# A two-attention kernel: V of the second attention in 4096 B rows, quads in pairs, one PSUM pool

## The chip, the core and the metric

The kernel runs on one core of a Trainium2 chip. Its time is the device time of that core in microseconds. The times and the profile are those of the kernel before the change.

## What is computed

Two attention blocks over cached keys and values, independent of each other, with their outputs side by side. All data are bf16.

```python
def _A_ref(x, k_cache, v_cache, wq, wo):      # x 16x32x1024, 32 query heads, 4 key/value heads, Sk 1024, Dh 128
    q = (x @ wq).reshape(B, Sq, Hq, Dh).transpose(0, 2, 1, 3)
    k = jnp.repeat(k_cache, rep, axis=1)      # rep = 8
    v = jnp.repeat(v_cache, rep, axis=1)
    scores = jnp.einsum("bhqd,bhkd->bhqk", q, k) * (Dh ** -0.5)
    p = softmax(scores, axis=-1)
    o = jnp.einsum("bhqk,bhkd->bhqd", p, v)
    return o.transpose(0, 2, 1, 3).reshape(B, Sq, Hq * Dh) @ wo
# _B_ref: the same with 32 key/value heads (no repeat)
return jnp.concatenate([a, b], axis=-1)
```

The second attention (B) reads K and V of 16 batches x 32 heads x 1024 x 128, 134 MB each; the first one (A) reads an eighth of that.

## The kernel before

**Quads.** Both attentions are cut into 128 units of 128 query rows, called quads. A quad of A is four heads of one batch that share K and V. A quad of B is two batches (`q.b0`, `q.b0 + 1`) times two heads (`q.h0`, `q.h0 + 1`), 32 queries each. For every quad the kernel makes scores into two PSUM banks, the negated row maximum (`st_max`, L866, DVE), the exponential with its sum (`st_exp`, L879, ACT), the transpose of P by TensorE with two bf16 taken as one fp32 (`st_ptr`, L891), its copy into `PT_sb` (`st_pev`, L540), the product with V (`st_pv`, L913 for A, L921 for B), the normalizing copy into `O_sb` (`st_norm`, L937 on ACT, L938 on DVE), a transpose of O (`st_otr`, L943) and its copy into `OTA_sb` or `OTB_sb` (L540). Query projections (L624, L643), the shuffling of B's queries into `QR` (L667) and the output projections (L712, added up by L723 and L726) run between the quads.

**B's K.** A tile `KB_sb` holds two heads of one batch: a partition has 16 consecutive keys, one row of 4096 B from memory (`st_dmaK`, L781). DVE transposes it in place in 32x32 blocks (`st_ktrB`, L815). Because of this layout the scores are made of 32x32 tiles of the matmul array, four passes of eight matmuls for each quad (L856): the row group is head and half (`rg = 2 * hh + g2`), the column group is batch and head (`cg = 2 * t_ + hh`). There are 8 K slots.

**B's V.** A V load (`st_dmaV`, L794) takes two heads of one batch with 8 consecutive keys to a partition and head, so a row from memory has 2048 B. A quad needs two such loads; there are 3 slots of two loads. In the product a stationary tile is 32 queries wide (128 rows x 32 columns, four column groups), the moving operand is one 128-key chunk of V, 128 columns.

**PSUM.** Two pairs of banks are for scores, taken in turn (`ps_s`); four banks are for everything else (`ps_g`), and two of them are kept for projections where possible.

**Order.** The program first lists all operations with what they read and write. `list_schedule` then plays them through with the durations in `DUR`, a model of the DMA queue (`PACKET`, `DMA_ISSUE`, `SP_AHEAD`), the slots in `SLOTS` and a priority made of the longest path and the step number; the order in which it starts the operations is the order in which each engine's instructions are written out. At run time there are only in-order engines and semaphores. All loads go through SP's queue, in one order; a load whose slot isn't free holds back all loads behind it. `evac` copies may go to ACT or DVE, as the planner chooses (`any`).

The main loop adds one quad of B (`quadB_all`) and about one of A (`quadA_all`) at each of 128 steps. `quadB_all` adds V's loads for the quad three ahead and K's loads for the quad four ahead.

Of the kernel before, what the change touches and what calls it, by code (L numbers as in the profile page):

```python
# [16 lines left out]
NVB_SLOTS = 3  # L17
NQT = 7
# [10 lines left out]
PE_MODE = {"scoresB": 2, "Qshuf": 2, "Qshuf2": 2, "PVB": 1}  # L29
MODE_SWITCH = 0.05  # L30
LOOK = 0.35
STEP_US = 3
STEP_NEAR = 0
TAIL_STEP = 123
# [11 lines left out]
    "scoresB": (0.216, 0.20), "scoresA": (0.216, 0.20), "PT_trA": (0.49, 0.22), "PT_trB": (0.49, 0.22), "PVA": (0.45, 0.22), "PVB": (0.112, 0.22),  # L46
    "OT_tr": (0.056, 0.22), "KTA_tr": (0.45, 0.22), "Qshuf": (0.15, 0.20), "Qshuf2": (0.15, 0.20), "qprojA": (0.432, 0.20), "qprojB": (0.432, 0.20),
    "oprojA": (0.432, 0.20), "oprojB": (0.432, 0.20), "xT_tr": (0.45, 0.22),
    "exp": (1.10, 0.12), "PT_ev@act": (0.466, 0.13), "norm@act": (0.25, 0.13), "OT_ev@act": (0.11, 0.13), "KTA_ev@act": (0.466, 0.13),
    "qA_ev@act": (0.47, 0.13), "qB_ev@act": (0.478, 0.13), "QR_ev@act": (0.478, 0.13), "acc0@act": (0.47, 0.13), "acc0@dve": (0.58, 0.12), "xT_ev@act": (0.90, 0.13),  # L50
    "o_fin@act": (0.47, 0.13),
    "KBt_tr": (1.126, 0.11), "max": (1.12, 0.11), "recip": (0.06, 0.11), "norm@dve": (0.23, 0.13), "PT_ev@dve": (0.58, 0.12),
    "OT_ev@dve": (0.08, 0.12), "KTA_ev@dve": (0.58, 0.12), "QBt_tr": (0.345, 0.10), "acc+": (0.58, 0.12), "accF": (0.59, 0.12),
# [4 lines left out]
PACKET = {"kb_dma": (4096, 0.159), "wqh_dma": (1024, 0.049)}  # L58
PACKET_DEFAULT = (2048, 0.084)
# [40 lines left out]
SLOTS = {"bank": 4, "P": 3, "PT": 3, "stat": 6, "O": 2}  # L100
BANK_RESERVE = {"pj": 2}


def actual(res):
    out = []
    for r in res:
        if not isinstance(r, Virt):
            out.append(r)
        elif r.cls == "bank":
            out.append(("bank", 4 + r.idx))  # L110
        else:
            out.append((r.cls, r.idx))
    return tuple(out)


class Prog:
# [118 lines left out]
    def list_schedule(self, lat=0.05, look=LOOK):  # L235
# [48 lines left out]

        def slot_time(i):

            t = 0.0
            for k_, v in enumerate(acq[i]):
                nth = sum(1 for w in acq[i][:k_] if w.cls == v.cls)
                idle = [slot_free[v.cls][x] for x in range(SLOTS[v.cls]) if held[v.cls][x] is None]  # L290
                keep = sum(k for kind, k in BANK_RESERVE.items() if kind != v.kind and not any(h is not None and h.kind == kind for h in held["bank"])) if v.cls == "bank" else 0
                if len(idle) <= keep + nth:
                    return None
                t = max(t, sorted(idle)[nth])
            return t

        def acquire(i, st):
            for v in acq[i]:
                x = min((x for x in range(SLOTS[v.cls]) if held[v.cls][x] is None), key=lambda x: slot_free[v.cls][x])
                held[v.cls][x] = v  # L300
                v.idx = x
# [25 lines left out]

        def occ(i, eng):
            return dict(ops[i].alts)[eng] if ops[i].alts else ops[i].dur
        while True:  # L330
            best = None
            bkey = None
            for eng, lst in ready.items():
# [11 lines left out]
                for i in lst:  # L345
                    s_ = slot_time(i) if acq[i] else 0.0
                    if s_ is not None:
                        at[i] = max(ready_t[i], fe, s_) + sw(i)
                if not at:
                    continue  # L350
                emin = min(at.values())
                cand = [i for i in at if at[i] <= emin + look]
# [21 lines left out]
            if op.dma_key is not None:  # L374
                free[beng] = st + DMA_ISSUE
                xs = max(st + DMA_FIRST, dma_free[0])
                dma_free[0] = xs + dma_time(op)
                op.t1 = dma_free[0] + DMA_LAST
            else:
                oc, tl = occ(best, beng)  # L380
                free[beng] = st + oc
                op.t1 = st + oc + tl
# [67 lines left out]
def build(nc, pa, pb, out):  # L450
# [34 lines left out]
    with stack:  # L485
# [21 lines left out]
        VB_sb = sb("VB_sb", [P, NVB, 2, 2, NCH, Dh], BF)  # L507
# [3 lines left out]
        P_sb = sb("P_sb", [P, SLOTS["P"], Sk], BF)  # L511
        PT_sb = sb("PT_sb", [P, SLOTS["PT"], NCH, P], BF)
        O_sb = sb("O_sb", [P, SLOTS["O"], Dh], BF)

        ps_s = ps("ps_s", [P, 2, 2, 512], F32)
        ps_g = ps("ps_g", [P, 4, 512], F32)

        def bank(v):
            return ps_g[:, v.idx, :]

        def bankb(v):
            return ps_g[:, v.idx, :].bitcast(BF)
# [229 lines left out]
        def mk_quadB(t):  # L752
# [7 lines left out]
            q.hp = jb % 2  # L760
            q.b0 = 4 * q.G + 2 * q.bp
            q.h0 = q.m * MS + 2 * q.hp
            q.ks = [(2 * t + t_) % NKB for t_ in range(2)]
            q.vslot = t % NVB
# [6 lines left out]
        def st_dmaK(q, t_=None):  # L771
            if q.pi == 0:
                if not q.kv_new:
                    return
                sl = q.kvslot
                pr.add("sp", lambda e: e.dma_start(KA_sb[:, sl, :, :], pa["k"][q.b, q.s].rearrange("(p c) d -> p c d", c=NCH)),
                       writes=[("KA", sl)], dma_key=f"ka{sl}", name="ka_dma", dur=Sk * Dh * 2, wtag={("KA", sl): q.kid})
            else:
                sl = q.ks[t_]
                ksrc = pb["k"][q.b0 + t_, q.h0:q.h0 + 2].rearrange("hh (p s) d -> (hh p) (s d)", s=16)  # L780
                pr.add("sp", lambda e: e.dma_start(KB_sb[:, sl, :], ksrc), writes=[("KB", sl)], dma_key=f"kb{sl}", name="kb_dma", dur=2 * Sk * Dh * 2, wtag={("KB", sl): q.kid})  # L781

        def st_dmaV(q):
            if q.pi == 0:
                if not q.kv_new:
                    return
                sl = q.kvslot
                pr.add("sp", lambda e: e.dma_start(VA_sb[:, sl, :, :], pa["v"][q.b, q.s].rearrange("(p c) d -> p c d", c=NCH)),
                       writes=[("VA", sl)], dma_key=f"va{sl}", name="va_dma", dur=Sk * Dh * 2, wtag={("VA", sl): q.kid})
            else:  # L790
                sl = q.vslot
                for t_ in range(2):
                    vsrc = pb["v"][q.b0 + t_, q.h0:q.h0 + 2].rearrange("hh (p c) d -> p hh c d", c=NCH)
                    pr.add("sp", lambda e, t_=t_, vsrc=vsrc: e.dma_start(VB_sb[:, sl, t_, :, :, :], vsrc), writes=[("VB", sl, t_)],  # L794
                           dma_key=f"vb{sl}_{t_}", name="vb_dma", dur=2 * Sk * Dh * 2, wtag={("VB", sl, t_): q.kid})
# [17 lines left out]
        def st_ktrB(q, t_):  # L813
            sl = q.ks[t_]
            pr.add("dve", lambda e: e.transpose(KB_sb[:, sl, :].bitcast(F32), KB_sb[:, sl, :].bitcast(F32)),  # L815
                   writes=[("KB", sl)], name="KBt_tr", rtag={("KB", sl): q.kid}, wtag={("KB", sl): ("T", q.kid)})

        s_rr = [0]

        class SBuf:  # L820
            def __init__(self, idx):
                self.idx = idx
                self.res = [("bank", 2 * idx), ("bank", 2 * idx + 1)]

        def st_scores(q):
            q.vS = SBuf(s_rr[0] % 2)
            s_rr[0] += 1
            q.vP, q.vPT, q.vst, q.vO = Virt("P"), Virt("PT"), Virt("stat"), Virt("O")
            q.vbt, q.vbo = Virt("bank"), Virt("bank")
            vS = q.vS  # L830
            if q.pi == 0:
# [3 lines left out]
                for u in range(2):  # L835
                    pr.add("pe", lambda e, u=u: e.matmul(ps_s[:, vS.idx, u, :], qt[:, q.b, q.hh0:q.hh0 + 4, :].rearrange("p a q -> p (a q)"),  # L836
                                                         KTA_sb[:, sl, u * 512:(u + 1) * 512], start=True, stop=True),
                           reads=[("QT", q.s % 2, q.hh0 + a) for a in range(4)] + [("KTA", sl)], writes=vS.res, name="scoresA", dur=0.225,
                           tag="A%d" % q.t, rtag=dict([(("QT", q.s % 2, q.hh0 + a), q.s) for a in range(4)] + [(("KTA", sl), q.kid)]))
            else:  # L840
                gp = (q.m * NG + q.G) % 2

                def e_s(e, fp):
                    last = None
                    if True:
                        f, pd = fp // 2, fp % 2
                        o0 = f * 64 + pd
                        for t_ in range(2):
                            a = 2 * q.bp + t_
                            for hh in range(2):  # L850
                                cg = 2 * t_ + hh
                                for g2 in range(2):
                                    rg = 2 * hh + g2
                                    lhsT = QR[32 * rg:32 * rg + 32, gp, a, q.hp, o0:o0 + 63:2]
                                    rhs = KB_sb[32 * rg:32 * rg + 32, q.ks[t_], :].rearrange("p (s x) -> p s x", s=16)[:, :, o0:o0 + 63:2]
                                    last = e.matmul(ps_s[32 * cg:32 * cg + 32, vS.idx, g2, :].rearrange("p (s j) -> p s j", s=16), lhsT, rhs,  # L856
                                                    start=(fp == 0), stop=(fp == 3), tile_position=(32 * rg, 32 * cg))
                    return last
                for fp_ in range(4):
# [296 lines left out]
```

## Time and profile before

| | |
|---|---|
| time, median of 3 runs (lowest to highest) | 888.49 us (888.01 to 891.52) |
| profiled execution: its own time, its span | 888.67 us, 886.9 us |
| granted TensorE clock | 0.994 |
| PE, DVE, ACT busy | 798.9 us (90%), 733.0 (83%), 612.1 (69%) |
| bytes moved by DMA, mean rate | 341.65 MB, 385 GB/s |
| DMA packets | 144830 |
| loads of B's V, of B's K | 256 x 512 KB each, issued by SP |

The span runs from the first to the last instruction; the time has 1.8 us around it. Busy shares are unions of an engine's instructions, and overlapping matmuls count once. PEld is TensorE's weight load. "SPq" in waits is SP's queue of DMA issues. A wait is given as who waited, at which line, for whom, with the sum in us, the number of times and the longest.

### The profile page before, as it was taken

The page shows a single profiled execution, that of the slowest core. Times are in us where ns is not written, and L with a number is a line of the kernel's source. Part 1 is how long each engine was busy: PE and PEld are TensorE (multiplying, and loading weights), DVE is VectorE, ACT ScalarE, POOL GpSimd, SP SyncE. Part 2 cuts the span into 40 slices and gives each one's busy share as a digit, 9 for nine tenths or more (in the row PEclk, how much of TensorE's full clock was granted, in tenths as well). Part 3 has the DMA queues.
Part 4 walks back from the last instruction along what each step waited for, and adds up shares of the span by engine and source line. Part 5 has one row for each costly group of instructions (what it writes and reads, how often), then busy time and mean ns, then how long its engine had stood idle before and what let it go on. Part 6 is the DMA issues. An engine that isn't in the chain of part 4 may idle for free.

```text
span 886.9 us, 29149 instructions
## 1 busy us (share of the span) xinstructions
PE 798.9 (90%) x12699; PEld 468.8 (53%) x12864; DVE 733.0 (83%) x1020; ACT 612.1 (69%) x1357; POOL 5.0 (1%) x15
## 2 busy tenths in 40 slices
PE   7999899998999999999999989998999877987976
PEld 3455555555555555555555555555555544554643
DVE  0498987979887888998898879887889888998985
ACT  3486886667777575767768666686667766676763
POOL 0000000000000000000000000000000000000000
PEclk9999999999999999999999999999999999999999
DMA  9999999999999999999999999999999999999995
GB/s 331 397 395 393 392 393 396 393 394 392 395 377 384 393 395 394 392 392 394 395 364 394 393 392 396 394 394 387 396 395 377 392 395 395 376 395 393 397 397 200
DMA packets 144830, 341.65 MB, mean 385 GB/s; under 512 B 12032, under 2 KB 12032, under 8 KB 144704
## 3 DMA queue, kind: packets, MB, share of 16 engines
q1 hardware_dynamic: 144144, 337.95, 100.6%
q8 instruction: 101, 1.65, 0.8%
q0 software_dynamic: 560, 1.84, 0.5%
q14 instruction: 25, 0.20, 0.1%
HBM read 337.64 MB, written 2.10 MB: 383 GB/s over the span
## 4 chain that ended last, share of the span: by engine, by line
PE 49%; DMA 21%; DVE 13%; ACT 11%; SPq 3%; issue 3%; DVEq 0%; ACTq 0%
DMA KB_sb<-in_B_k_cache_dram 14%; PE ps_s L856 11%; PE ps_g L712 9%; PE ps_g L891 8%; ACT P_sb L879 7%; DVE stat L866 6%; DVE KB_sb L815 5%; DMA VA_sb<-in_A_v_cache_dram 5%; PE ps_g L921 4%; PE ps_g L624 4%; PE ps_g L913 4%; PE ps_g L643 3%; PE ps_s L836 2%; ACT PT_sb L540 2%; PE ps_g L943 2%
## 5 line engine op out<-in xcount | busy, mean ns | idle before, releaser
L866 DVE TENSOR_REDUCE stat<-ps_s 128x1 f32<-128x1024 f32 x256 | 305.5, 1209 | 56.1 <-PE ps_s L856 49.8
L815 DVE STREAM_TRANSPOSE KB_sb<-KB_sb 128x1024 f32<-128x1024 f32 x256 | 309.3, 1228 | 38.0 <-DMA KB_sb<-in_B_k_cache_dram 36.3
L879 ACT ACTIVATE P_sb<-ps_s,stat 128x1024 bf16<-128x1024 f32 x256 | 285.8, 1118 | 55.3 <-DVE stat L866 53.4
L891 PE MATMUL ps_g<-id,P_sb 128*128 128x128 f32 x1024 | 172.4, 296 | 13.6 <-ACT OTA_sb L540 5.7
L856 PE MATMUL ps_s<-KB_sb,QR 32*32 32x512 bf16 x4096 | 160.9, 397 | 17.9 <-ACT P_sb L879 13.9
L891 PEld LDWEIGHTS ps_g<-id,P_sb 128*128 128x128 f32 x1024 | 148.7, 207 | 49.6 <-ACT OTA_sb L540 8.7
L540 ACT COPY PT_sb<-ps_g 128x512 f32<-128x512 f32 x235 | 136.2, 591 | 44.9 <-PE ps_g L891 43.8
L937 ACT ACTIVATE O_sb<-ps_g,stat 128x128 bf16<-128x128 f32 x193 | 70.1, 371 | 67.8 <-PE ps_g L921 40.5
L921 PE MATMUL ps_g<-VB_sb,PT_sb 128*32 128x128 bf16 x4096 | 90.6, 222 | 5.7 <-ACT PT_sb L540 1.7
L856 PEld LDWEIGHTS ps_s<-KB_sb,QR 32*32 32x32 bf16 x4096 | 48.2, 89 | 77.2 <-ACT P_sb L879 21.0
L921 PEld LDWEIGHTS ps_g<-VB_sb,PT_sb 128*32 128x32 bf16 x4096 | 59.7, 97 | 52.1 <-issue 37.5
L913 PE MATMUL ps_g<-VA_sb,PT_sb 128*128 128x128 bf16 x1024 | 78.6, 221 | 5.8 <-DMA VA_sb<-in_A_v_cache_dram 2.8
L913 PEld LDWEIGHTS ps_g<-VA_sb,PT_sb 128*128 128x128 bf16 x1024 | 61.0, 98 | 35.2 <-issue 14.6
L643 PE MATMUL ps_g<-wq_sb,xT_sb 128*128 128x512 bf16 x230 | 68.2, 393 | 5.2 <-DMA wq_sb<-in_B_wq_dram 2.3
L712 PE MATMUL ps_g<-woB_sb,OTB_sb 128*128 128x512 bf16 x230 | 62.6, 380 | 8.8 <-ACT OTB_sb L540 2.3
L836 PE MATMUL ps_s<-KTA_sb,QT_sb 128*128 128x512 bf16 x180 | 64.2, 385 | 5.4 <-ACT O_sb L937 2.6
L712 PE MATMUL ps_g<-woA_sb,OTA_sb 128*128 128x512 bf16 x238 | 59.0, 380 | 4.0 <-issue 1.7
L943 PE MATMUL ps_g<-ident,O_sb 128*128 128x128 bf16 x256 | 51.5, 223 | 8.3 <-ACT O_sb L937 4.4
L879 ACT ACTIVATION_READ_ACCUMULATOR P_sb<-ps_s,stat 128x1 f32 x256 | 51.4, 201 | 0.0
L624 PE MATMUL ps_g<-xT_sb,wq_sb 128*128 128x512 bf16 x174 | 49.1, 380 | 2.0 <-issue 1.0
L540 ACT COPY OTA_sb<-ps_g 128x64 f32<-128x64 f32 x120 | 25.7, 214 | 33.2 <-PE ps_g L943 32.5
L723 DVE TENSOR_TENSOR acc<-acc,ps_g 128x512 f32<-128x512 f32 x64 | 40.8, 673 | 9.1 <-PE ps_g L712 8.9
(44 smaller groups left out, 511.6 us busy)
## 6 DMA issues: line engine op xcount, KB each, us to landing
VB_sb<-in_B_v_cache_dram SPq DMA_DIRECT2D x256, 512.0 KB, 12.2
KB_sb<-in_B_k_cache_dram SPq DMA_DIRECT2D x256, 512.0 KB, 12.4
KA_sb<-in_A_k_cache_dram SPq DMA_DIRECT2D x64, 256.0 KB, 12.3
VA_sb<-in_A_v_cache_dram SPq DMA_DIRECT2D x64, 256.0 KB, 12.2
wq_sb<-in_B_wq_dram SPq DMA_DIRECT2D x16, 512.0 KB, 12.1
woB_sb<-in_B_wo_dram SPq DMA_DIRECT2D x32, 256.0 KB, 11.2
woA_sb<-in_A_wo_dram SPq DMA_DIRECT2D x32, 256.0 KB, 9.9
wq_sb<-in_A_wq_dram SPq DMA_DIRECT2D x12, 512.0 KB, 12.6
```

The costliest lines, as they stand in the source:

```text
L540: return e.copy(dst, src) if hasattr(e, "activation") else e.tensor_copy(dst, src)
L624: last = e.matmul(bank(v)[:, 0:tn], w_[:, j, hh * Dh:(hh + 1) * Dh], xT_sb[:, 0, j, t0:t0 + tn], start=(j == 0), stop=(j == DJ - 1))
L643: last = e.matmul(bank(v)[:, 0:CW], xT_sb[:, 1, j, G * P:(G + 1) * P], wq_sb[:, j, mh * CW:(mh + 1) * CW], start=(j == 0), stop=(j == DJ - 1))
L712: last = e.matmul(bank(v)[:, 0:OUTW], OT[:, gp, hh, :], wo_[:, hh, oh * OUTW:(oh + 1) * OUTW], start=(hh == 0), stop=(hh == nh - 1))
L815: pr.add("dve", lambda e: e.transpose(KB_sb[:, sl, :].bitcast(F32), KB_sb[:, sl, :].bitcast(F32)), writes=[("KB", sl)], name="KBt_tr", rta ...
L836: pr.add("pe", lambda e, u=u: e.matmul(ps_s[:, vS.idx, u, :], qt[:, q.b, q.hh0:q.hh0 + 4, :].rearrange("p a q -> p (a q)"), KTA_sb[:, sl, ...
L856: last = e.matmul(ps_s[32 * cg:32 * cg + 32, vS.idx, g2, :].rearrange("p (s j) -> p s j", s=16), lhsT, rhs, start=(fp == 0), stop=(fp == 3 ...
L866: pr.add("dve", lambda e: e.tensor_reduce(stat[:, vst.idx, 0:1], ps_s[:, vS.idx, :, :], AXIS.XY, ALU.max, negate=True), writes=vS.res + [v ...
L879: return e.activation(dst, src, ACTF.Exp, bias=stat[:, vst.idx, 0:1], scale=1.0, accum_out=stat[:, vst.idx, 1:2])
L891: last = e.transpose(bank(vb)[:, m * P:(m + 1) * P], p32[:, m:Sk // 2:NPK], id32[:])
L913: last = e.matmul(bank(vb)[:, 0:Dh], ptc_of(vPT, c, 0, P), VA_sb[:, kvs, c, :], start=(c == 0), stop=(c == NCH - 1))
L921: last = e.matmul(bank(vb)[32 * a:32 * a + 32, 0:Dh], ptc_of(vPT, c, 32 * a, 32 * a + 32), VB_sb[:, kvs, a // 2, a % 2, c, :], start=(c == ...
```

## The change

- **V of B.** A V load now has K's layout: two heads of one batch, 16 consecutive keys to a partition, one row of 4096 B. The number of loads (256) and their size (512 KB) stay. A V tile thus holds two heads of equal place on different halves of the partitions (64 partitions a head).
- **Pairs.** Two quads that follow each other become a pair with a common set of four K tiles and four V tiles. The quads of a pair no longer split the heads as (0,1) and (2,3): `q.e` is the parity, and a quad has heads `e` and `2 + e` of both batches. The scores of both quads are one operation of four passes of 16 matmuls, each on a 32x32 tile of its own. The exponentials of both quads go into one tile `P2_sb`; its eight transposes give two PT copies into `PT2_sb`; the product with V takes 64 matmuls of 64x64 tiles whose moving operand is 256 columns wide (two V tiles side by side).
- **Turning O back.** Each quad's result now holds, for each row, both heads of a parity, of which half is wanted. `st_norm` copies 256 columns instead of 128, and the transpose becomes two matmuls with `rowsel`, a selecting identity that POOL fills at the start. The copy into `OTB_sb` is 128 columns of bf16 instead of 64 fp32 words.
- **Slots.** V: 6 slots of one load, filled behind the pair's product (`pairB`). P2 and PT2 have one slot each, O2 three; P and PT go from 3 to 2, `stat` from 6 to 8, the projected queries (`NQT`) from 7 to 5.
- **PSUM.** One pool of 8 banks; scores take banks in neighbouring pairs, at most 6 at a time; a pair of quads takes four at once.
- **Planner.** New durations, a larger cost for a change of the array's tiling, a model of instruction blocks that PE has to fetch, and rules for placing banks (`place`).

```diff
-NVB_SLOTS = 3
-NQT = 7
+NVB_SLOTS = 6
+NQT = 5
...
-SLOTS = {"bank": 4, "P": 3, "PT": 3, "stat": 6, "O": 2}
-BANK_RESERVE = {"pj": 2}
+SLOTS = {"bank": 8, "P": 2, "P2": 1, "PT": 2, "PT2": 1, "stat": 8, "O": 2, "O2": 3}
...
-        VB_sb = sb("VB_sb", [P, NVB, 2, 2, NCH, Dh], BF)
+        VB_sb = sb("VB_sb", [P, NVB, 16, Dh], BF)
...
-        ps_s = ps("ps_s", [P, 2, 2, 512], F32)
-        ps_g = ps("ps_g", [P, 4, 512], F32)
+        psum = ps("psum", [P, 8, 512], F32)
...
+        pr.add("pool", lambda g: g.memset(rowsel[:], 0.0), writes=["rowsel"], name="c0")
+        for r_ in range(4):
+            pr.add("pool", lambda g, r_=r_: g.tensor_copy(rowsel[32 * r_:32 * r_ + 32, r_ % 2, 32 * r_:32 * r_ + 32], ident[32 * r_:32 * r_ + 32, 32 * r_:32 * r_ + 32]),
+                   reads=["ident"], writes=["rowsel"], name="c1")
...
-                for t_ in range(2):
-                    vsrc = pb["v"][q.b0 + t_, q.h0:q.h0 + 2].rearrange("hh (p c) d -> p hh c d", c=NCH)
+        def tile_src(key, x):
+            q, i = quadsB[2 * (x // 4)], x % 4
+            h = q.m * MS + 2 * (i % 2)
+            return pb[key][q.b0 + i // 2, h:h + 2].rearrange("e (p s) d -> (e p) (s d)", s=16)
...
+        def st_scoresB(qs):
...
+                for x in range(4):
+                    for q in qs:
+                        for g2 in range(2):
+                            r0 = 32 * (2 * q.e + g2)
+                            lhsT = QR[r0:r0 + 32, gp, 2 * q.bp + x // 2, x % 2, o0:o0 + 63:2]
+                            rhs = KB_sb[r0:r0 + 32, q.ks[x], :].rearrange("p (s x) -> p s x", s=16)[:, :, o0:o0 + 63:2]
+                            last = e.matmul(bank(q.vS[g2])[32 * x:32 * x + 32, :].rearrange("p (s j) -> p s j", s=16), lhsT, rhs,
+                                            start=(fp == 0), stop=(fp == 3), tile_position=(r0, 32 * x))
...
+        def st_pvB(qs):
...
+                for c in range(c0, c0 + 4):
+                    for t_ in range(2):
+                        s0 = q0.vs[2 * t_]
...
+                        for q in qs:
+                            e0, n0 = 64 * q.e, 64 * t_
+                            last = e.matmul(bank(q.vbo)[n0:n0 + 64, 0:2 * Dh].rearrange("p (i d) -> p i d", i=2), pt[e0:e0 + 64, c // 2, n0:n0 + 64, c % 2],
+                                            VB_sb[e0:e0 + 64, s0:s0 + 2, c, :], start=(c == 0), stop=(c == 15), tile_position=(e0, n0))
...
+                def e_ot(e):
+                    for i in range(2):
+                        last = e.matmul(bank(vb)[:, 256:384], O2_sb[:, vO.idx, i, :], rowsel[:, i, :], start=(i == 0), stop=(i == 1))
...
+        def pairB(n):
+            qs = [quadsB[2 * n], quadsB[2 * n + 1]]
+            for x in range(4):
+                st_ktrB(4 * n + x)
...
+            st_scoresB(qs)
+            for x in range(4):
+                st_dmaKB(4 * n + NKB + x)
+            for q in qs:
+                st_max(q)
+                st_exp(q)
+            st_ptB(qs)
+            st_pvB(qs)
+            for x in range(4):
+                st_dmaVB(4 * n + NVB + x)
+            for q in qs:
+                st_recip(q)
+                st_norm(q)
+                st_otr(q)
```

More of the change, by code (lines that the diff above doesn't have):

```diff
@@ L285, in slot_time @@
         def slot_time(i):
-            t = 0.0
+            got = place(i)
+            if got is None:
+                return None
+            t = got[1]
             for k_, v in enumerate(acq[i]):
[L289 to L294, printed above, removed]
+                if v.cls != "bank":
+                    nth = sum(1 for w in acq[i][:k_] if w.cls == v.cls)
+                    idle = [slot_free[v.cls][x] for x in range(SLOTS[v.cls]) if held[v.cls][x] is None]
+                    if len(idle) <= nth:
+                        return None
+                    t = max(t, sorted(idle)[nth])
@@ L295, in slot_time @@
             return t
         def acquire(i, st):
+            got = iter(place(i)[0])
             for v in acq[i]:
-                x = min((x for x in range(SLOTS[v.cls]) if held[v.cls][x] is None), key=lambda x: slot_free[v.cls][x])
+                if v.cls == "bank":
+                    x = next(got)
+                else:
+                    x = min((x for x in range(SLOTS[v.cls]) if held[v.cls][x] is None), key=lambda x: slot_free[v.cls][x])
                 held[v.cls][x] = v
@@ L332, in list_schedule @@
             bkey = None
+            waiting = [i for i in ready.get("pe", ()) if banks_of(i) > 1 and ready_t[i] <= free.get("pe", 0.0) + HOLD_AHEAD]
+            big[0] = max(waiting, key=lambda i: bl[i]) if waiting else None
             for eng, lst in ready.items():
@@ L769, in mk_quadB @@
             return q
[L771 to L781, printed above, removed]
@@ L839, in st_scores @@
                            tag="A%d" % q.t, rtag=dict([(("QT", q.s % 2, q.hh0 + a), q.s) for a in range(4)] + [(("KTA", sl), q.kid)]))
[L840 to L859, printed above, removed]
-                    pr.add("pe", lambda e, fp_=fp_: e_s(e, fp_), reads=[("QR", gp, 2 * q.bp), ("QR", gp, 2 * q.bp + 1), ("KB", q.ks[0]), ("KB", q.ks[1])],
-                           writes=vS.res, name="scoresB", dur=0.275, tag="B%d" % q.t,
-                           rtag={("QR", gp, 2 * q.bp): (q.m, q.G), ("QR", gp, 2 * q.bp + 1): (q.m, q.G), ("KB", q.ks[0]): ("T", q.kid), ("KB", q.ks[1]): ("T", q.kid)})
@@ L864, in st_max @@
         def st_max(q):
             vS, vst = q.vS, q.vst
-            pr.add("dve", lambda e: e.tensor_reduce(stat[:, vst.idx, 0:1], ps_s[:, vS.idx, :, :], AXIS.XY, ALU.max, negate=True),
-                   writes=vS.res + [vst], name="max")
+            pr.add("dve", lambda e: e.tensor_reduce(stat[:, vst.idx, 0:1], both(vS), AXIS.XY, ALU.max, negate=True),
+                   writes=vS + [vst], name="max")
         def st_exp(q):
```

346 lines of the change are left out of this document (218 added, 128 removed).

## The prediction

> **What bounds the kernel now.** I read the page's 40 slices first, then SP's part of the timeline at the start and the windows beside it, then the groups, SP's own waits and the end of the timeline.
>
> The slices: the 16 DMA engines are full in all but the last, at 364 to 397 GB/s.
>
> ```profile
> DMA  9999999999999999999999999999999999999995
> GB/s 331 397 395 393 392 393 396 393 394 392 395 377 384 393 395 394 392 392 394 395 364 394 393 392 396 394 394 387 396 395 377 392 395 395 376 395 393 397 397 200
> ```
>
> PE (90% busy) and DVE (83%) are close behind, and the chain that ended last gives DMA only 21%; but a chain passes through whichever engine releases a buffer, while full queues in every slice mean that bytes arrive no sooner whatever the engines do. So the question is what a byte costs. The timeline of SP shows in which order loads are queued at the start: six V tiles of the second attention, four K tiles, four small ones (left out), four K tiles again.
>
> ```profile
> 10.44 9.01 SPq L794 DMA_DIRECT2D VB_sb<-in_B_v_cache_dram  x6
> 19.50 3.76 SPq L781 DMA_DIRECT2D KB_sb<-in_B_k_cache_dram  x4
> ...
> 25.91 5.37 SPq L781 DMA_DIRECT2D KB_sb<-in_B_k_cache_dram  x4
> ```
>
> They land in that order, some 9 us later: 3.1 MB of V are 8 us, 2.1 MB of K 5 us, 1 MB 3 us, 2.1 MB of K 5 us. The windows cut there (columns: stretch, length, POOL, clock, DMA share, GB/s):
>
> ```profile
> 20.00:28.00 8.00, 0.00 (x0) 1.00 1.05 386
> 28.00:33.00 5.00, 0.00 (x0) 1.00 1.03 409
> 33.00:36.00 3.00, 0.00 (x0) 1.00 1.04 390
> 36.00:41.00 5.00, 0.00 (x0) 1.00 1.04 410
> ```
>
> V and the small loads have rows of 2048 B, K has rows of 4096 B: 386 to 390 against 409 to 410 GB/s at the same engine share. That is the price the change touches. Next the groups that it rewrites (mean ns of one, then idle before it):
>
> ```profile
> L856 PE MATMUL ps_s<-KB_sb,QR 32*32 32x512 bf16 x4096 | 160.9, 397 | 17.9 <-ACT P_sb L879 13.9
> ...
> L937 ACT ACTIVATE O_sb<-ps_g,stat 128x128 bf16<-128x128 f32 x193 | 70.1, 371 | 67.8 <-PE ps_g L921 40.5
> L921 PE MATMUL ps_g<-VB_sb,PT_sb 128*32 128x128 bf16 x4096 | 90.6, 222 | 5.7 <-ACT PT_sb L540 1.7
> ```
>
> 4096 matmuls of 397 ns make 160.9 us busy: many tiles run at once. Then SP's waits (us, times, longest) and V's own line (ns and us, minimum/median/maximum):
>
> ```profile
> SPq L794 <- PE ps_g L921: 73.9, 39, 5.1
> SPq L794 <- PE ps_s L856: 41.8, 30, 5.3
> L794 SPq DMA_DIRECT2D VB_sb<-in_B_v_cache_dram x256: 368/888/3098, 10.4 to 868.9; - x128
> ...
> DMA to landing us min/median/max: 7.1/12.2/15.0
> ```
>
> SP does stand before V's buffers, and the engines stay full through it, since some 10 us of loads are queued: the one output that SP sends on an idle queue lands after 2.1 us. Last the end: all loads are issued by 869.4, the last PV starts at 879.61, the output leaves at 883.40.
>
> ```profile
> 859.93 9.46 SPq L794 DMA_DIRECT2D VB_sb<-in_B_v_cache_dram  x6
> ...
> 879.61 0.63 PE L921 MATMUL ps_g<-VB_sb,PT_sb 128*32 128x128 bf16 x32
> ...
> 883.40 0.36 SPq L729 DMA_DIRECT2D out_dram<-acc  x1
> ```
>
> **The change part by part.** The sum is made against the profiled run, 888.67 us (span 886.9 and 1.8 around it); the median is 888.49, the same within 0.2.
>
> *Rows of V.* 256 loads of 512 KB are 134.2 MB. At 386 GB/s they take 347.7 us, at 409.5 they take 327.7: 20.0 us less. As a check, all the queue's 337.95 MB at these rates are 134.2/409.5 + 203.7/386 = 855 us, and loads run from 2.5 to about 878, so some 20 us are the first slice's ramp, short dips and the thin end; I leave those as they are. Ends: 386 may be 2 GB/s off either way, and so may 409 (18 to 22 us). [...]
>
> *Scores (PE).* Now 32 matmuls per quad take 1.13 us (timeline at 399.90), eight tiles at a time; a pair then takes 2.26. After, 64 matmuls on sixteen tiles at once. Floor: their weight loads, 32 in 0.60 us now, so 1.20; ceiling: 2.26, no more overlap than now. I take 1.25, since L856 and L921 both overlap as far as their tiles differ: −1.0 per pair.
>
> *PV (PE).* Now 32 matmuls of 128 columns, four tiles at a time, take 0.63 us, of which 0.22 is the last one's own time: 13 ns each. After, 64 of 256 columns in 64x64 tiles: four at a time 26.5 ns each, 1.9 us with the end, against 1.26 for two quads: +0.65. If only two ran at a time it is 3.6, +2.35. I take four, by the nearest row. [...]
>
> *Turning O back (PE).* Two selecting matmuls per quad for one transpose (223 ns): about 0.29, +0.12 per pair. PE in sum: −0.2 per pair, −15 us in 64 pairs; ends −19 and +158 (no gain in scores, two tiles in PV). It is beside the loads: PE idles 88 us, 68 in a span of 868.
>
> *Evictions (ACT, DVE).* L540 takes 214 ns for 64 columns and 591 for 512, 0.84 ns a column. Normalizing 256 columns for 128 adds 0.11, the copy of 128 for 64 adds 0.05: 21 us in 128 quads, three quarters on ACT (612 busy, then 628 of 868, 72%), the rest on DVE (733 to 738, 85%). Hidden by their idle time; uncovered, 21 us at most. Maxima, exponentials, K transposes, transposes of P and PT copies keep number and size.
>
> *Banks, P2/PT2 with one slot, NQT 5, planner.* From exponentials to the end of a pair's PV are about 2×1.3 + 2×0.75 + 0.6 + 1.9 = 6.6 us of a period of 13.1 ((880−47)/63.5), so single slots don't close the loop. A pair takes four score banks at once; waits for score banks (PE on L879) are 50 us now and lie under the loads. The new order itself can't be read from this trace: zero, with the 8 us of dips in the slices (377, 364, 377, 376) as what order can win or lose.
>
> *V's buffers.* Six 4096 B slots as before, but filled and freed by pairs of four: half the next pair's V is queued only when this pair's PV is done. Behind a waiting V load stand all of SP's later loads (K, A's K and V, weights), so SP blocks longer and the queue runs shorter. Loop: 0.9 us issue + landing + 1.9 us PV must fit a period of 12.9, so landing may be 10.1. It is 12.2 now, with 10 of it queue; while SP waits that drains, and 7.1 has been seen. Zero, since the engines stay fed as long as some of the queue is left. A longer loop is a rival below.
>
> *Start.* The first scores start at 40.6, when all four K tiles needed have been in for 7 us: 0, up to +2. POOL's five small instructions are ahead of that.
>
> *End.* PV of a whole pair, 1.9 for 0.63, +0.2 in norm, turn and copy: +1.5. The last two V tiles wait for the last pair but one: 0 to 3, I take 0.5. Together +2.
>
> Sum: 888.5 − 20.0 + 2.0 = 870.5.
>
> **The rivals.** *V's ring closes (slower).* If V still landed 12.2 us after issue, the loop would be 15.0 us: 47 + 63×15.0 + 11 = 1003. The queue gives way first, so I price half of it, landing at 11.1: 13.9 us, 934. It decides from a landing over 10.1. For it: 73.9 us of SP's waits are on PV already. Against: those waits never emptied the engines, and a planner orders both sides. Chance 0.10.
>
> *PE becomes the bound (slower).* Two 64x64 tiles at a time, scores gaining: +1.5 per pair, 799 + 96 = 895 busy, with some 10 us of ends 905. It decides from +0.9 per pair (58 us, the idle less the ends). For it: 90% busy, and no row has this tile. Against: both packed shapes here overlap fully. Chance 0.07.
>
> *Bytes, not rows (no change).* If a byte cost the same in either row, as where memory and not the engine's packet sets the rate, the term of the rows is zero and the time 888.5 + 2 = 890.5. Against it, 386 and 409 GB/s in stretches that follow each other. [...] Chance 0.03.
>
> *The coarser steps give half back.* A pair needs four K and four V landed instead of two; 0.15 us lost per pair is 10 us: 880, between 876 and 888. Chance 0.14, 0.10 of it under 884.
>
> **How the numbers follow.** The forecast has 0.66. A measurement here tells 0.5% (4.4 us) from no change. Faster: 0.66 + 0.10 = 0.76. Same: 0.03 + 0.04 = 0.07. Slower: 0.10 + 0.07 = 0.17. The forecast's own range is 863 (−22, and 4 us of dips gone) to 877 (−18, start and end at their ends). The 8-in-10 range reaches over the half-back case and the unchanged one to 893 and leaves out the two slower ones.
>
> **What would show it.** V's landing loads at about 409 GB/s and slices near 400; fewer packets by 32,768; scores of a pair near 1.25 us and PV near 1.9; V's landing under 10 us with SP's waits on PV longer; DMA still 9 in all slices but the last. Wrong if slices fall under 390, if DVE or ACT wait long for PV or scores, or if PV of a pair takes 3 us.

## The result, and the profile after

The changed kernel takes 884.67 us (median of 6 runs, 883.7 to 885.22) beside 888.57 us for the kernel before: 0.995 of it, 95% interval 0.9936 to 0.9965. That is 3.9 us less, where 18 were forecast. The profiled execution took 884.66 us, its span is 882.9 us, its granted clock 0.989 (0.988 to 0.992 over the six runs) where the kernel before had 0.994.

First the changed kernel's slices of DMA and GB/s, its packets, and the chain's shares by engine:

```profile
DMA  9999999999999999899999999999999999999984
GB/s 337 414 409 391 383 409 400 382 411 391 410 386 392 415 413 398 324 411 394 364 367 412 411 413 351 409 407 407 406 379 414 404 404 380 396 411 403 363 332 176
...
DMA packets 112063, 341.66 MB, mean 387 GB/s; under 512 B 12032, under 2 KB 12032, under 8 KB 111936
...
PE 55%; DVE 19%; ACT 19%; DMA 4%; issue 2%; SPq 0%; ACTq 0%
```

The best slices went from 397 to 415 GB/s, but 15 of the 40 are now under 392 where 8 were, and the DMA's share of the chain fell from 21% to 4%. The loads can come faster, and something else holds them back. SP's waits say what (us, times, longest), and the third line gives V's time to landing:

```profile
SPq L892 <- PE psum L1044: 118.0, 39, 10.7
SPq L868 <- PE psum L905: 80.6, 35, 6.3
...
DMA to landing us min/median/max: 3.5/7.7/15.1
```

SP stands before V's buffers for 118.0 us instead of 73.9, and before A's K (L868) for another 80.6. V lands after 7.7 us instead of 12.2: less is queued. The engines' groups that the change rewrote:

```profile
L1044 PE MATMUL psum<-VB_sb,PT_sb 64*64 64x256 bf16 x4096 | 129.1, 275 | 13.6 <-ACT P_sb L978 6.6
L1062 ACT ACTIVATE O_sb<-psum,stat 128x128 bf16<-128x128 f32 (+1 forms) x202 | 80.4, 413 | 49.2 <-PE psum L1044 24.0
L954 PE MATMUL psum<-KB_sb,QR 32*32 32x512 bf16 x4096 | 79.8, 394 | 6.3 <-ACT P_sb L978 2.6
```

The scores (L954) are busy 79.8 us, half of the 160.9 before: a pair takes 1.25 us (79.8/64). The product with V (L1044) is busy 129.1 us for 90.6. L1062's second form, the normalizing of 256 columns, takes 474 ns where 128 columns take 371. Last the end, from the chain in order of time (start, length, what):

```profile
855.95 3.59 PE psum L1044 x49
859.54 0.02 issue
859.55 0.33 SPq L892
859.88 0.04 issue
859.92 6.25 DMA VB_sb<-in_B_v_cache_dram
866.17 0.14 issue
866.30 1.97 PE psum L1044 x64
868.27 0.02 issue
868.29 0.33 SPq L892
868.62 0.04 issue
868.66 4.65 DMA VB_sb<-in_B_v_cache_dram
873.31 0.14 issue
873.45 1.97 PE psum L1044 x64
```

A V tile uses the slot of the tile six before it, and a pair has four tiles. So the last two tiles of every pair wait for the product of the pair before. At the end the chain goes twice through product, issue, landing, product: 6.25 and 4.65 us of waiting for a landing.

### The profile page after: what moved, and what is told of

The parts are those of the page before. It is cut to its first block, busy times and chain, and to the rows that moved or that the text cites. A ratio compares the mean times of both kernels' runs of the same rounds, so it can differ in the third digit from the quotient of the medians.

```text
span 882.9 us, 29603 instructions
## 1 busy us (share of the span) xinstructions
PE 798.5 (90%) x12992; PEld 525.0 (59%) x12992; DVE 739.5 (84%) x1034; ACT 618.1 (70%) x1343; POOL 6.1 (1%) x20
## 4 chain that ended last, share of the span: by engine, by line
PE 55%; DVE 19%; ACT 19%; DMA 4%; issue 2%; SPq 0%; ACTq 0%
ACT P_sb L978 13%; DVE stat L965 10%; PE psum L1044 10%; PE psum L805 8%; PE psum L954 7%; DVE KB_sb L913 6%; PE psum L1024 5%; PE psum L990 5%; PE psum L736 4%; PE psum L717 4%; PE psum L932 4%; PE psum L1010 3%; ACT PT_sb L633 2%; PE psum L905 2%; DMA KB_sb<-in_B_k_cache_dram 2%
## 5 line engine op out<-in xcount | busy, mean ns | idle before, releaser
L965 DVE TENSOR_REDUCE stat<-psum 128x1 f32<-128x1024 f32 x256 | 302.7, 1212 | 71.4 <-PE psum L954 37.8
L978 ACT ACTIVATE P_sb<-psum,stat 128x1024 bf16<-128x1024 f32 x256 | 286.1, 1119 | 86.3 <-DVE stat L965 82.2
L633 ACT COPY PT_sb<-psum 128x512 f32<-128x512 f32 x236 | 137.6, 595 | 46.9 <-PE psum L990 23.4
L1044 PE MATMUL psum<-VB_sb,PT_sb 64*64 64x256 bf16 x4096 | 129.1, 275 | 13.6 <-ACT P_sb L978 6.6
L1044 PEld LDWEIGHTS psum<-VB_sb,PT_sb 64*64 64x64 bf16 x4096 | 110.2, 109 | 33.7 <-issue 30.5
L1062 ACT ACTIVATE O_sb<-psum,stat 128x128 bf16<-128x128 f32 (+1 forms) x202 | 80.4, 413 | 49.2 <-PE psum L1044 24.0
L990 PE MATMUL psum<-id,P_sb 128*128 128x128 f32 x512 | 90.4, 301 | 8.2 <-ACT P_sb L978 5.2
L1024 PE MATMUL psum<-id,P_sb 128*128 128x128 f32 x512 | 87.1, 293 | 6.2 <-ACT P_sb L978 2.7
L932 PE MATMUL psum<-KTA_sb,QT_sb 128*128 128x512 bf16 x256 | 83.1, 383 | 6.7 <-ACT P_sb L978 4.7
L990 PEld LDWEIGHTS psum<-id,P_sb 128*128 128x128 f32 x512 | 72.3, 209 | 28.0 <-ACT P_sb L978 16.7
L1024 PEld LDWEIGHTS psum<-id,P_sb 128*128 128x128 f32 x512 | 69.8, 194 | 26.9 <-ACT P_sb L978 7.5
L954 PE MATMUL psum<-KB_sb,QR 32*32 32x512 bf16 x4096 | 79.8, 394 | 6.3 <-ACT P_sb L978 2.6
L954 PEld LDWEIGHTS psum<-KB_sb,QR 32*32 32x32 bf16 x4096 | 45.1, 89 | 34.7 <-issue 7.3
```

The lines of the kernel that those rows point to most:

```text
L633: return e.copy(dst, src) if hasattr(e, "activation") else e.tensor_copy(dst, src)
L932: pr.add("pe", lambda e, u=u: e.matmul(bank(vS[u]), qt[:, q.b, q.hh0:q.hh0 + 4, :].rearrange("p a q -> p (a q)"), KTA_sb[:, sl, u * 512:(u ...
L954: last = e.matmul(bank(q.vS[g2])[32 * x:32 * x + 32, :].rearrange("p (s j) -> p s j", s=16), lhsT, rhs, start=(fp == 0), stop=(fp == 3), t ...
L965: pr.add("dve", lambda e: e.tensor_reduce(stat[:, vst.idx, 0:1], both(vS), AXIS.XY, ALU.max, negate=True), writes=vS + [vst], name="max")
L978: return e.activation(dst, src, ACTF.Exp, bias=stat[:, vst.idx, 0:1], scale=1.0, accum_out=stat[:, vst.idx, 1:2])
L990: last = e.transpose(bank(vb)[:, m * P:(m + 1) * P], p32[:, m:Sk // 2:NPK], id32[:])
```

## The experiments

Each ratio is to the kernel before, run beside it on the same chip (medians 888.6 to 889.4 us). Theories: the rows' length made the gain (the forecast's term); the engines' own pace lies just below the loads and stops the gain; the end takes some of it back; and, formed after the first results, where a row starts in SBUF sets its price.

### Rows alone, and the loads taken away

**e1: the kernel before with V in 4096 B rows**, everything else as it was. The keys of V are then in another order than the probabilities; the instructions and their order are those of before.

```diff
-pb["v"][..., q.h0:q.h0 + 2].rearrange("hh (p c) d -> p hh c d", c=NCH)
+pb["v"][..., q.h0:q.h0 + 2].rearrange("hh (p s) d -> (hh p) (s d)", s=16)
```

> The kernel before, its order of instructions unchanged, with only the rows of B's V made 4096 B (the keys of V then stand in another order than P's, which the output shows and the time does not). Theory 1, the engines have a pace of their own not far under 888 us, which the slower loads had covered: the rows alone give about what the whole change gave, 880 to 886 us, and SP waits for buffers far more than before. Theory 2, the six V slots filled by pairs take the gain back: without pairs the rows give all of it, 866 to 871 us.

Measured: 878.35 us, 0.9879 [0.9862, 0.9895], between the two expected ranges and nearer to the first. Its slices of DMA and GB/s, and its SP waits:

```profile
DMA  9999999999999999999999999999998999999994
GB/s 318 403 400 402 398 397 405 402 396 399 404 363 372 405 401 404 403 399 404 404 372 389 401 401 404 402 404 398 405 403 333 401 402 404 403 405 402 407 407 184
```

```profile
SPq L794 <- PE ps_g L921: 252.9, 81, 8.8
```

The rows alone gain 11 us (V's window from 20 to 28 us shows 406 GB/s for 386), and then SP waits 252.9 us for the product with V to free buffers, against 73.9. The DMA digits are still 9 in nearly every slice, so a 9 does not say that the loads bind. The change as a whole gains less than this one part of it.

**e2: the changed kernel with V in 2048 B rows.**

```diff
-tile_src("v", x)       # "e (p s) d -> (e p) (s d)"
+tile_src2(x)           # "e (p c) d -> p e c d"
```

> The changed kernel, its order unchanged, with the rows of B's V back at 2048 B (keys of V again out of order). Theory 1: the loads bound it again as before the change, 886 to 893 us. Theory 2: the pair's loop gets longer by the slower V loads on top of its waits, 895 to 905 us.

Measured: 883.0 us, 0.9931 [0.9916, 0.9946], under both expected ranges: taking the long rows away costs nothing. So in the changed kernel the rows' length isn't what gained. Its 2048 B rows ran at 406 GB/s (26 to 31 us), not 386; this was the first sign that the price of 386 belonged to something else.

**e3, e4: the loads of K and V after the first fill carry half their bytes**, in the kernel before and in the changed one.

```diff
-e.dma_start(KB_sb[:, sl, :], ksrc)
+e.dma_start(KB_sb[:, sl, 0:kn], ksrc[:, 0:kn])      # kn = 8 * Dh; V likewise
```

> The kernel before, order unchanged, where each K and V load of B after the first fill of its slot brings half its bytes in 2048 B rows (the rest of the tile keeps older data): about 134 MB less, so that loads can't bound it. What is left is the pace of the engines in that order. Theory 1: 870 to 885 us. Theory 2 says nothing against a much lower time, under 860.

> The changed kernel, order unchanged, with the same halved K and V loads of B. Theory 1: the time hardly moves, 872 to 884 us, though the engines' queues stand empty a third of the time. Theory 2: half the next pair's V lands some 3 us sooner after this pair's PV, so the loop of 64 pairs shortens and the time falls under 862 us.

Measured: e3 878.25 us, 0.9873 [0.9858, 0.9887]; e4 877.29, 0.9859 [0.9841, 0.9877]. In e3:

```profile
PE 816.6 (93%) x12864; PEld 469.1 (53%) x12864; DVE 727.0 (83%) x1020; ACT 611.1 (70%) x1357; POOL 5.0 (1%) x15
...
DMA  9987785859569685796747967679556966676761
...
PE 65%; DVE 18%; ACT 13%; issue 2%; DMA 1%; SPq 1%; ACTq 0%; DVEq 0%
```

With the DMA engines a third idle (a DMA share of 0.72 from 50 to 650 us and 0.67 from there to 860) the old order still takes 878 us. This is the pace of the engines; it lies only 11 us under the kernel before, and faster loads can't buy more than that. The first line also corrects a reading: here PE has all of its 12864 matmul records and is busy 816.6 us. The page of before shows 12699 of 12864 (PEld has them all), so its 88 us of idle PE are some 18 too many.

e4 is 7.4 us under the changed kernel: with all its loads that order does not reach its engines' pace. Where those 7 us go is taken up under "The end".

### Which engine sets that pace

**e5, e6, e7: e3 with one engine's work cut**: half of the chunks in both products with V (PE), the maximum over half of the columns (DVE), the exponentials over half of the columns (ACT).

```diff
-for c in range(NCH):                       # e5, both products
+for c in range(0, NCH, 2):
-ps_s[:, vS.idx, :, :], AXIS.XY, ALU.max    # e6
+ps_s[:, vS.idx, :, 0:256], AXIS.XY, ALU.max
+src, dst = src[:, 0:1], dst[:, 0:1]        # e7 (and 0:Dh // 2 for A)
```

> The kernel before with halved K and V loads of B (878.25 us), order unchanged, where the products with V of both attentions take only the even chunks of keys: 2048 + 512 matmuls fewer, about 60 us of PE's busy time; all else as it was. Theory 1, the pace under the loads is PE's in-order stream: the time falls by 25 to 60 us, to 818 to 853. If instead the loop over DVE and ACT sets the pace, it falls by less than 10.

> The same kernel with halved loads, all PV matmuls there, and the row maxima taken over half the columns (256 of 512 in each bank): about 140 us of DVE's 727 busy fewer. Theory 1, PE's stream is the pace: it falls by less than 15 us, to no less than 863. If DVE sets the pace: under 840.

> The same kernel with halved loads and the exponentials taken over half the columns (the other half of P is filled once at the start): about 130 us of ACT's 611 busy fewer. Theory 1: falls by less than 15 us. If ACT, through the score banks it frees, sets the pace: under 850.

Measured: e5 863.48 us, 0.9712 [0.9693, 0.9732]; e6 860.41, 0.9678 [0.9658, 0.9697]; e7 862.13, 0.9697 [0.9678, 0.9717]. The busy times, e3 against each: PE 816.6 and 754.8, DVE 727.0 and 600.2, ACT 611.1 and 513.1. So 62, 127 and 98 us less work (e5's page lacks 144 of 10304 matmul records; at the 18 us for 165 above, its 62 is more like 46) give 15, 18 and 16 us: a quarter to a third, a seventh and a sixth of what was cut. The theory that PE's stream alone is the pace asked for 25 us or more from e5 and for less than 15 from e6 and e7, and falls; DVE alone (under 840) and ACT alone (under 850) fall too. What is left is that the three share the pace, each waiting for the others in turn (in e3 DVE waits 60.0 us for the scores, ACT 47.9 for the maxima, PE's weight loads 16.8 for the exponentials); which of these waits set the pace was not followed.

### The end

**e8: the changed kernel with its last two V tiles (254 and 255) in K's slots 0 and 1**, free by then, so that they needn't wait for the pair before.

```diff
+if x >= LATE and x < 2 * NIT:              # LATE = 2 * NIT - 2
+    sl = x - LATE
+    pr.add("sp", lambda e: e.dma_start(KB_sb[:, sl, :], tile_src("v", x)), writes=[("KB", sl)], ...)
...
+if 4 * n + 8 == 2 * NIT:                   # queued behind the last pair's K
+    st_dmaVB(LATE); st_dmaVB(LATE + 1)
```

> The changed kernel, complete, with only the last two V tiles placed in K slots that are free once the last pair but one has its scores, so that they need not wait for that pair's product with V. The order differs in the last pairs only. Theory 1, as far as the end goes: the chain through V's slots at the end (two issues, each landing 5 to 6 us later with empty queues) is cut once, 879 to 882 us. If the end is bound by the engines anyway: 884 to 886.

Measured: 877.5 us (876.67 to 881.61), 0.9883 [0.9855, 0.991], under the 879 to 882 expected. The two loads leave early (SP's timeline: start, length, line), and the chain at the end no longer passes through a landing:

```profile
846.70 0.80 SPq L894 DMA_DIRECT2D KB_sb<-in_B_v_cache_dram  x2
854.69 2.80 SPq L898 DMA_DIRECT2D VB_sb<-in_B_v_cache_dram  x4
```

```profile
861.47 1.93 PE psum L1055 x64
863.40 0.64 PE psum L1030 x4
...
866.30 1.90 PE psum L1055 x64
```

The two last products start 4.8 us apart instead of 7.15. The medians differ by 7.2 us, but not all of that is the end. The same maximum, the 251st of 256, comes just before e8's two loads leave. In DVE's timeline of the changed kernel, then of e8, it opens these rows:

```profile
848.39 4.58 DVE L965 TENSOR_REDUCE stat<-psum 128x1 f32<-128x1024 f32 x4
```

```profile
844.89 3.45 DVE L971 TENSOR_REDUCE stat<-psum 128x1 f32<-128x1024 f32 x3
```

From there to the end of the span are 34.5 us in the changed kernel and 30.8 in e8: the end gives 3.7 us, and e8's run was 3.5 us ahead before it began.

**e9, e10, e11, e12: the same end with 2048 B rows, with half loads, and once more; and the changed kernel once more.** e9 adds e2's edit to e8, e10 adds e4's, e11 is e8, e12 is the changed kernel.

```diff
-KB_sb[:, sl, :], tile_src("v", x)                                              # e9, e8's two loads
+KB_sb[:, sl, :].rearrange("p (e c d) -> p e c d", e=2, c=NCH), tile_src2(x)
-KB_sb[:, sl, :], tile_src("v", x)                                              # e10
+KB_sb[:, sl, 0:8 * Dh], tile_src("v", x)[:, 0:8 * Dh]
```

> The changed kernel with the last two V tiles in K slots (877.5 us), order unchanged, with the rows of B's V at 2048 B (keys of V out of order). Theory 1, the engines' own pace holds it once the end is mended: 876 to 881 us, the rows worth less than 3. If the loads still held it: their 20 us come back, 890 to 898.

> The same kernel with the last two V tiles in K slots and with halved K and V loads of B: the pace of the engines in the order of pairs without the chain at the end. Theory 1: 870 to 876 us, so at most some 6 us under the kernel with full loads. If V's slots still held it in mid-run: under 866.

> The changed kernel with the last two V tiles in K slots, once more, for its difference to the changed kernel on the same chip. If the end's chain is what that kernel loses: 4 to 8 us faster than it, 876 to 880. If the first measurement was a lucky one: within 2 us of it.

> The changed kernel as it is, on the same chip as the one with the end mended: 883 to 886 us by its earlier runs, under either theory.

Measured: e9 878.63 us, 0.9889 [0.9856, 0.9923]; e10 875.84, 0.984 [0.9813, 0.9868]; e11 879.57, 0.9879 [0.9863, 0.9896]; e12 884.13, 0.9936 [0.9909, 0.9963]. By medians the mended end is worth 4.6 us here (e12 less e11) and 7.2 between e8 and the changed kernel's first runs. But the runs of e9, e11 and e12 spread over 7 to 8 us and overlap (e11 877.34 to 884.92, e12 879.72 to 887.78), so the traces say more: from the 251st maximum to the end are 33.4 us in e12 and 30.2 in e11. With the 34.5 and 30.8 above, the end is worth some 3.5 us (2.6 to 4.3). e9 beside e8 and e11 shows no cost of the shorter rows within that spread. e10 puts the pace of the engines in the new order at 876, some 2 us under the old one's, with runs from 871.82 to 877.99; differences of 2 us among these are not read.

What the spread goes with is the granted clock: e12's three runs at 0.993 to 0.996 take 879.72 to 880.12 us, its six at 0.988 to 0.992 take 881.2 to 887.78. e4's trace splits the 7.4 us between it and the changed kernel: it reaches the 251st maximum at 843.39 us, 5.0 us sooner, and takes 2.6 us less from there on. For the 5.0 us before the end the traces show two candidates: the changed kernel's clock of 0.989 against 0.993, and its DVE waiting for K to land (us, times, longest, from 50 to 848.39 us), of which e4's trace shows nothing in that stretch:

```profile
DVE KB_sb L913 <- DMA KB_sb<-in_B_k_cache_dram: 4.3, 4, 1.7
```

No run separates the two.

### Where a row starts

e2 and e9 have the loads of the kernel before in rows of the same length, but no price of 386 GB/s. What differs is where V's rows begin in SBUF: `stat` went from 6 slots to 8, 32 bytes a partition more, and it lies ahead of the large tiles. They began 224 bytes past a multiple of 256 and now begin on one (`VB_sb` at byte 175072 of a partition, then at 173056).

**e13: the kernel before with 8 slots' room for `stat`**, and nothing else; it still uses 6.

```diff
-stat = sb("stat", [P, SLOTS["stat"], 4], F32)
+stat = sb("stat", [P, 8, 4], F32)
```

**e14: e9 with a pad that puts the starts back to 224. e15: the changed kernel with that pad.**

```diff
+sb("pad", [P, 56], F32)
```

**e16: the kernel before with room for 12** (starts 64 past a multiple of 256). **e17: with room for 16** (128 past).

> The kernel before, complete, order unchanged, where only the tile stat has 128 B a partition instead of 96 (two slots that nothing uses), so that all tiles behind it in SBUF start at multiples of 256 B as in the changed kernel, and not 32 B short of one. Theory A, the start of a row in SBUF costs time for each row: V's loads (2048 B rows) move at some 406 GB/s for 386 and K's at 417 for 409, the loads drop by some 30 us and the engines' own pace of 877 to 879 us is left. If the place doesn't matter (the order of SP's queue or its depth made the rate): 887 to 890.

> The changed kernel with the last two V tiles in K slots and V in 2048 B rows (878.63 us, keys of V out of order), order unchanged, with a pad of 224 B behind stat, so that all later tiles start 32 B short of a multiple of 256 B, as in the kernel before. Theory A: 2048 B rows fall back to some 386 GB/s, the loads bind it again and it goes to 885 to 893. If the place doesn't matter: 877 to 880.

> The changed kernel, complete, order unchanged, with the same pad of 224 B. Theory A: rows of 4096 B fall to some 409 GB/s and the others to 387; the loads take some 15 us more and are still under the pace of the order with V's chain at its end, so the time rises by 2 to 6 us, to 886 to 890. If the place doesn't matter: 883 to 886.

> The kernel before, order unchanged, with stat at 192 B, so that later tiles start 64 B past a multiple of 256 B. Under theory A it tells the step: if 64 B is enough, V's loads move at 406 GB/s and the time is 877 to 880; if the step is 128 or 256 B, 386 GB/s and 887 to 890.

> The kernel before, order unchanged, with stat at 256 B, so that later tiles start 128 B past a multiple of 256 B. Theory A with a step of 256 B: V's loads at 387 GB/s and 886 to 889 us, as with 64 B. With a step of 128 B: 406 GB/s and 877 to 879 us, as with full multiples of 256 B.

Measured: e13 877.63 us, 0.9869 [0.9851, 0.9886]; e14 895.78, 1.007 [1.0053, 1.0087]; e15 886.82, 0.9977 [0.9962, 0.9992]; e16 886.81, 0.9972 [0.9958, 0.9986]; e17 886.29, 0.9968 [0.9942, 0.9993].

The prediction read 386, 409 and 410 GB/s in three windows of before, the first with V's rows of 2048 B and the others with K's of 4096 B (columns: stretch, length, POOL, clock, DMA share, GB/s). The same windows of e13:

```profile
20.00:28.00 8.00, 0.00 (x0) 1.00 1.05 406
28.00:33.00 5.00, 0.00 (x0) 1.00 1.03 418
...
36.00:41.00 5.00, 0.00 (x0) 1.00 1.03 418
```

and of e16, whose starts moved as well but not to a multiple of 256:

```profile
20.00:28.00 8.00, 0.00 (x0) 1.00 1.05 386
28.00:33.00 5.00, 0.00 (x0) 1.00 1.04 406
...
36.00:41.00 5.00, 0.00 (x0) 1.00 1.04 407
```

e17 gives 387, 406 and 405. (e14 came out 3 us above the end of what was expected.) So 32 bytes in front of a tile are worth 20 GB/s to V's rows and 9 to K's, and 11.4 us of the time; 96 or 160 bytes are worth nothing in these rates. In the changed kernel's order the stretch from 26 to 31 us is V's. That window in turn of the changed kernel (4096 B rows on the multiple), e15 (4096 B, off it), e9 (2048 B, on it) and e14 (2048 B, off it):

```profile
26.00:31.00 5.00, 0.00 (x0) 1.00 1.03 420
```

```profile
26.00:31.00 5.00, 0.00 (x0) 1.00 1.03 410
```

```profile
26.00:31.00 5.00, 0.00 (x0) 1.00 1.05 408
```

```profile
26.00:31.00 5.00, 0.00 (x0) 1.00 1.05 388
```

The times follow the rates only until the engines' pace is reached: 895.78 us at 388 GB/s (e14), 878.63 at 408 (e9), 877.5 and 879.57 at 420 (e8, e11), all with the mended end. Long rows and good starts can stand in for each other: either brings V to 406 GB/s and the kernel before to 878 us (e1, e13). What the second adds in that order was not run; in the order of pairs with the mended end it is not seen (e9 beside e8 and e11). In the changed kernel, with its rows long already, the starts are worth 2 to 3 us (e15 beside 884.67 and 884.13), no more than the runs of one kernel differ there.

The fastest kernels that do the whole work are thus e8 (877.5 us, as e11 879.57) and e13 (877.63), 5 to 7 us under the changed kernel and 10 to 12 under the one before. They tie; e13 gets there with one number of the old kernel.

## Why the prediction was wrong

*Rows of V, −20.* Failed as the first term, in two ways. **The gain was taken whole.** The prediction held that full queues in every slice mean that bytes arrive no sooner whatever the engines do. They were full because SP keeps some 10 us of loads queued (before, V lands 12.2 us after its issue, an output on an idle queue after 2.1); e1's are full too, at the engines' pace. The engines, fed at once, need 878 us (e3), so the most that any load could gain was 11, and e1, which changes the rows and nothing else, gained 11. **The price was not that of the row's length alone.** Most of the step from 386 to 409 can be had with the old rows: where they start on the multiple they run at 406 (e13). As supply the change did more than forecast: at 420 for 386 V's 134.2 MB take 28 us less, and K's as many, at 418 for 409 as in e13, another 7. The time shows a third of that at most.

*The rival "bytes, not rows"* had its cause half right and its conclusion wrong. With good starts, rows of 2048 and 4096 B differ by 3% in rate (406 and 418) and not visibly in time (e9, e8, e11). With the starts of before they differ as the windows said.

*PE, −15 us beside the loads.* Sizes right: scores 1.25 us a pair as taken, the product 1.97 for 1.9 (four tiles at a time, as forecast), the two selecting matmuls 0.30 for 0.29; PE is busy 798.5 us against 816.6, −18. That it idles 68 us as cover was misread from the records missing on the page, and the idle was not free: e5 to e7 show that PE, DVE and ACT wait for each other, and that less work on any of them shortens the kernel once the loads don't hold it. Of the 18 us the pace gained about 2 (e10 beside e3), which is within the spread of e10's runs.

*Evictions, +21 us hidden.* The sizes came: on ACT the normalizing went from 371 to 474 ns and the copy from 214 to 281, 0.17 us a quad or 22 in 128. In all ACT has 6.0 us more and DVE 6.5, 12.5 together, since DVE's maxima and K transposes took 8.2 less. By e6 and e7 some 2 us of such work would show where loads don't cover it (6.0/6 + 6.5/7): under a pace so near, "hidden" was too strong.

*V's buffers, zero; the rival of the ring 0.10.* In the middle the loop of issue, landing and product stays inside the period as the queue runs shorter (landing 7.7 us, SP's wait 118.0), as the paragraph on V's buffers had it. **At the end it closes.** There little other work lies between two pairs, and the loop becomes the period (7.15 us between the last two products). The prediction's term for it, the last two V tiles at 0.5 (0 to 3), measured some 3.5 (2.6 to 4.3, from the traces of the changed kernel, e8, e11 and e12), by the measure of what mending it gains. The rival had the mechanism and not the place.

*Sum as the runs have it.* 888.5, less 11 down to the engines' pace, plus some 3.5 for the end: 881. 884.67 was measured; the 3 to 4 us that are left lie before the end and go with the lower granted clock or with DVE's waits for K, and their cause stays open. The sum is made from the runs after the fact and foretells nothing.

*What was to show it.* V's rate (420 for about 409), 32,767 packets fewer, the times of scores and product, landing under 10 us and SP's longer waits all came. Two signs went against it: the DMA digits show an 8 in two slices ahead of the last, and 13 slices are under 390 GB/s, which the prediction named as a sign of being wrong (8 were before the change). The signs that came show the steps and not the time: each of them is also what one sees when loads have become faster than their users.

**Open.** Which chains among PE, DVE and ACT make up the 876 to 878 us was not taken apart further. Why the changed order gets a lower granted clock, and what that alone costs, is open. So is why e16 and e17 are 2 to 3 us faster than before, with V in that window at the rate of before and K below it. The old order with both long rows and good starts was not run; e3 says that it would find the same pace.

## What to carry to other kernels

Before a faster transfer is priced, find the pace under it: the same kernel with half the bytes in its loads, or a large sum of SP's waits for buffers, says how much of the gain can be kept (here e3's 878 us and e1's 252.9 us of waits), and full queues don't (e1's DMA digits). When a change resizes any tile, look at where the tiles behind it now start; a gain or loss seen after it may come from there, and putting back the start alone tells (here e13: 32 bytes, 11.4 us). A ring of buffers that holds less than two steps' loads (here six slots for four tiles a pair) may be hidden in the middle by other work and has to be priced at the drain, where that work is gone (here some 3.5 us).

## What the runs showed of the hardware

Rows that start 64, 128 or 224 bytes past a multiple of 256 in SBUF took each DMA engine some 4 ns longer here than rows that start on one, at 2048 B and at 4096 B alike. That is an estimate from the windows' rates: with the 16 engines full (DMA share 1.03 to 1.05), a 2048 B row takes 2048 x 16 / 386 = 84.9 ns at 386 GB/s (before) and 80.7 at 406 (e13); a 4096 B row takes 159.8 at 410 (e15) and 156.0 at 420 (the changed kernel). Starts at 64, 128 and 224 past the multiple cost V's rows alike (386, 387 and 386 GB/s in e16, e17 and before). All good starts here are multiples of 1024 as well, so the runs do not tell a step of 256 from one of 512 or 1024. What in such a start takes the 4 ns was not shown.

In the changed kernel 64 matmuls of 256 columns on 64x64 tiles of the matmul array take 1.97 us from first to last, of which 0.27 is the last one's own time (275 ns, L1044). That is (1.97 - 0.27) / 63 = 27 ns for each, twice the 13 ns that the prediction works out for 128 columns with four tiles at a time; by this estimate the 64x64 tiles run four at a time too, and two at a time would have taken 3.6 us. Sixteen 32x32 tiles at once halve the time of the scores (79.8 us busy for 160.9) with the same 4096 matmuls, of 394 ns for 397.
